# A second-layer weight pair loaded with unequal shares for the DMA engines

## The chip, the cores and the metric

The kernel runs on one core of a Trainium2 chip. The metric is the device time in microseconds (us) of one execution; for a kernel with several runs it is their median. A core has five engines that matter here: TensorE (PE; its weight loads are PEld), VectorE (DVE), ScalarE (ACT), GpSimd (POOL) and SyncE (SP), and sixteen DMA engines that move data between the chip's memory and the on-chip buffers. GpSimd and SyncE only issue the transfers here, apart from a few mask operations on GpSimd at the start.

## What is computed

Two layers follow each other. The first is attention over 8 batches, 8 heads, 576 positions and head dimension 64, with a window of 32 positions: the plain last 32 in heads 0 to 3, every fourth of the last 128 in heads 4 to 7. The second is a soft mixture of experts over the 4608 tokens that come out of it, with 8 experts of 4 slots:

```python
logits = x @ phi                          # 4608 x 32
d = softmax(logits, axis=0)               # over the tokens
slot_input = (d.T @ x).reshape(8, 4, 512)
for e in range(8):
    h = np.maximum(slot_input[e] @ w1[e], 0.0)     # w1[e]: 512 x 1024
    slot_out[e] = h @ w2[e]                        # w2[e]: 1024 x 512
c = softmax(logits, axis=1)               # over the slots
out = c @ slot_out.reshape(32, 512)       # 4608 x 512
```

All inputs and the output are f32 in memory. The weights w1 and w2 are 16.8 MB each, and q, k and v together 28.3 MB.

## The kernel before, in words

The program is a list of operations. Each names its engine, what it reads and writes, a cost and a key. A planner (`schedule`, lines 170 to 271) goes through them in its own modelled time, picks for each engine what can start first (the key decides between near ones), and so fixes the order of the instructions on every engine. The operations on GpSimd and SyncE keep the order in which the program lists them. `emit` (273 to 313) then writes the instructions, with semaphore waits where one engine needs another or a transfer. A DMA's semaphore is raised by each of the sixteen DMA engines, and a wait is for all of them (lines 303 to 307).

The attention is cut into eight units (two batches by four heads). A unit's q, k and v are loaded by six transfers of 32 rows (`load_unit`, line 411), into one of three staging buffers `stg`, with a cast from f32 to bf16 on the way. TensorE transposes them into `TT` (551 and 546), multiplies (589, 643), and VectorE and ScalarE work between. When a pair of units is through, the token logits (698), their exponentials and the slot sums (729, 746) follow.

The expert weights are loaded by `wload` (437 to 451), on GpSimd's queue as well, between and after the units. Their places: seven of the eight w1 matrices have buffers of their own (`WD`), the eighth and the w2 matrices go into staging buffers and `TT` as these come free. A w2 "pair" holds two experts: 128 rows (2 experts by 64 groups of 16 matrix rows), and in each row 16 x 512 f32 values that lie one after another in memory. The pairs are p0, p1, p2 and p3, the last cut by columns into p3a and p3b. GpSimd's order at the end is w15, w16, w17, p3a, p0, p1, p2, p3b (lines 760 to 788). Loads that reuse a buffer wait for TensorE to have read it.

p0 goes into `stg[:, 0, 0:8192]` (line 457). Line 449 cuts it into two loads of 128 rows by 4096 values:

```python
cut = [slice(0, 8), slice(8, 16)] if name == "p0" else [slice(None)]
```

After the last unit TensorE makes the slot inputs (798), the first expert layer (817), transposes (837), and the second layer (864), which takes the parts in the order p3a, p0, p1, p2, p3b, each waiting for its own load. Row sums (880) lie between p1 and p2. The result is scaled (891, 895), and the output is made tile by tile: TensorE multiplies (923, 925), VectorE and ScalarE scale out of PSUM (937, 938), and SyncE issues six output transfers (946). The first part of p0's buffer serves there as a staging tile (904 to 907).

Where the planner sees TensorE idle between the two times of `FILL` (line 24, in the planner's own us), it puts in filler: matmuls whose result nobody reads (`filler`, 950 to 966; line 955 in the profile), which keep TensorE busy.

Of the kernel before, what the change touches and what calls it, by code (L numbers as in the profile page):

```python
# [20 lines left out]
NU = 8  # L21
QB = 96
HALO = 32
FILL = (118, 148)


class DmaSem:
# [102 lines left out]
class Prog:  # L130
# [7 lines left out]
    def op(self, e, fn, r=(), w=(), a=(), alloc=(), cost=0.5, key=0.0, mode="f",  # L138
           sem=None, nbytes=0, nd=0, nq=1, ni=2, after=()):
        o = Op(e, fn, cost, key, mode)  # L140
        deps = list(after)
        for b in r:
            deps += b.ready
        for b in w:
            b.fresh()
            deps += b.prev
        for b in a:
            deps += b.prev
        seen = set()
        for d in deps:  # L150
            if d.id not in seen:
                seen.add(d.id)
                o.deps.append(d)
        for b in r:
            b.reads.append(o)
        for b in list(w) + list(a):
            b.ready.append(o)
        o.wr = [b for b in list(w) + list(a) if b.pool is not None]
        for b in list(r) + list(w) + list(a):
            if b.pool is not None and b not in o.touch:  # L160
                b.left += 1
                o.touch.append(b)
        o.alloc = list(alloc)
        o.sems = sem
        o.ni = ni + 2
        o.dma = nbytes / 435e3 + 0.011 * nd / 16 + 0.022 * nq
        self.ops.append(o)
        return o
# [147 lines left out]
def bass_dilated_sliding_attn__then__soft_moe_slots_kernel(  # L316
# [12 lines left out]
    op = P.op  # L329

    def sb(name, shape, dt=BF16):
        return A(nc.sbuf_tensor(name, shape, dt))
# [3 lines left out]
    stg = sb("stg", [128, 3, 9216])  # L336
# [22 lines left out]
    h_sb = sb("h_sb", [128, FF])  # L359
    hT = sb("hT", [128, 16, 128])  # L360
    half = sb("half", [128, 2, 32])
    so_sb = sb("so_sb", [128, DM])

    ps = A(nc.psum_tensor("ps", [128, 8, 512], F32))
# [19 lines left out]
    def pair(t):  # L384
        return ps[:, t.phys[0]:t.phys[0] + 2, :]
# [11 lines left out]
    b_stg = [Buf() for _ in range(3)]  # L397
# [5 lines left out]
    b_half = Buf()  # L403
    b_siT, b_h, b_hT, b_so = Buf(), [Buf(), Buf()], [Buf(), Buf()], [Buf(), Buf()]

    PACE = 8.26

    def due(u, x):
        return u * PACE + x

# [17 lines left out]
    HOME = {}  # L428
    b_home = []

    def home(ap, al, name):
        b = Buf()
        b.al = al
        HOME[name] = (ap, b)
        b_home.append((ap, b))

    def wload(name):
        ap, b = HOME[name]
        b.prev = [o for al in b.al for o in al.ready + al.reads]
        sem = DmaSem(nc, f"s_{name}")  # L440
        if name[:2] == "w1":
            src = moe_w1[int(name[2:])].rearrange("(p c) f -> p c f", c=4)
            dst = ap.rearrange("p (c f) -> p c f", c=4)
        else:
            g = int(name[1])
            c = {"": slice(0, 16), "a": slice(0, 8), "b": slice(8, 16)}[name[2:]]
            src = moe_w2[2 * g:2 * g + 2].rearrange("e (p c) f -> (e p) c f", c=16)[:, c, :]
            dst = ap.rearrange("p (c f) -> p c f", f=512)
        cut = [slice(0, 8), slice(8, 16)] if name == "p0" else [slice(None)]
        op("pool", lambda g: [g.dma_start(dst[:, x], src[:, x]) for x in cut], after=b.prev, a=[b],  # L450
           cost=0.6 * len(cut), sem=sem, nbytes=512 * ap.shape[1], nd=128 * len(cut), nq=len(cut))

# [1 line left out]
        home(WD[:, e, :], [], f"w1{e}")  # L454
    home(stg[:, 2, 0:4096], [b_stg[2]], "w17")
    home(stg[:, 2, 4096:8192], [b_stg[2]], "p3a")
    home(stg[:, 0, 0:8192], [b_stg[0]], "p0")
    home(stg[:, 1, 0:8192], [b_stg[1]], "p1")
    TTf = TT[:].rearrange("p a x -> p (a x)")
    home(TTf[:, 0:8192], b_TT, "p2")  # L460
# [35 lines left out]
    for i, t in enumerate(VNt):  # L496
# [6 lines left out]
       cost=0.1, key=1)  # L503
# [258 lines left out]
    for u in range(NU):  # L762
        for j in range(4):
            st_T(u, j)
        if u + 3 < NU:
            for n_ in W_AFTER.get(u + 2, ()):
                wload(n_)
            load_unit(u + 3)
        else:
            if u == 5:  # L770
                for n_ in W_AFTER[7]:
                    wload(n_)
            for n_ in {5: ["w17", "p3a"], 6: ["p0"], 7: ["p1"]}[u]:
                wload(n_)
        for i in range(6):
            st_S(u, i)
        for g in range(4):
            st_V(u, g)
        for g in range(4):
            st_P(u, g)  # L780
        for bpar in range(2):
            for x in range(2):
                st_X(u, bpar, x)
        if u % 2:
            for bpar in range(2):
                st_L(u - 1 + bpar, u)
# [25 lines left out]
    for hh in range(2):  # L812
        def pe(t, hh=hh):
            for c in range(4):
                for hi in range(2):
                    for j in range(4):
                        i_ = t.matmul(pair(hp)[32 * j:32 * j + 32, hh, :], siT[:, 512 * hi + 128 * c + 32 * j:
                                                       512 * hi + 128 * c + 32 * j + 32],
                                      w1v[2 * j + hi][:, c, 512 * hh:512 * hh + 512],
                                      start=(c == 0 and hi == 0), stop=(c == 3 and hi == 1))  # L820
            return i_
        ffn1 = op("pe", pe, r=[b_siT] + w1b, a=[hp], w=[b_hp[hh]], alloc=[hp] if hh == 0 else [],
                  cost=1.8, mode="c", key=K1, ni=64)
# [32 lines left out]
    PARTS = [("p3a", 3, 0, 8), ("p0", 0, 0, 16), ("p1", 1, 0, 16), ("p2", 2, 0, 16),  # L856
             ("p3b", 3, 8, 16)]
    for k_, (name, g, c0, c1) in enumerate(PARTS):
        wv = HOME[name][0].rearrange("p (c f) -> p c f", c=c1 - c0)
        for h_ in range(2):  # L860
            def pe(t, k_=k_, g=g, c0=c0, c1=c1, h_=h_, wv=wv):
                for c in range(c0, c1):
                    j = c % 4
                    i_ = t.matmul(pair(sp_)[32 * j:32 * j + 32, h_, 0:256],
                                  hT[:, c, 24 * g:24 * g + 32],
                                  wv[:, c - c0, 256 * h_:256 * h_ + 256],
                                  start=(k_ == 0 and c < c0 + 4), stop=(k_ == 4 and c >= c1 - 4))
                return i_
            last_ = op("pe", pe, r=b_hT + [HOME[name][1]], alloc=[sp_] if k_ == h_ == 0 else [],
                       a=[sp_, b_sp[h_]], cost=0.13 * (c1 - c0) / 4, mode="c",  # L870
                       ni=2 * (c1 - c0),
                       key=K1 + 2 + 0.5 * k_ + 0.1 * h_)
            if k_ == 2:
                mid = last_
    rs = tile(psum, 1)

    def rsum(t):
# [6 lines left out]
       after=[mid])  # L884
    op("dve", lambda vv: vv.reciprocal(rtok[:], bank(rs)[:, 0:N_TOK // 128]), r=[rs], w=[b_rtok],
       cost=0.2, key=K1 + 1)
# [23 lines left out]
    for o, (t0, n) in enumerate(TILES):  # L910
# [4 lines left out]
        for j0 in range(0, n, 2):  # L915
# [4 lines left out]
            for j in range(2 if split else min(2, n - j0)):  # L920
                def pe(t, o=o, po=po, j0=j0, j=j, split=split):
                    if split:
# [4 lines left out]
                p0 = op("pe", pe, r=(b_so[j:j + 1] if split else b_so) + b_expT, a=[po],  # L927
                        w=[b_po[j]], alloc=[po] if j == 0 else [], after=[p0] if j else [],
                        cost=0.12 if split else 0.22, key=kk + 0.01 * j)
                col = rcol[o] + (0 if split else j0 + j)  # L930

                def ev(en, po=po, ost=ost, j=j, j0=j0, split=split, col=col):
# [3 lines left out]
                    if en is nc.scalar:  # L936
# [3 lines left out]
                        cost=0.35 if split else 0.6, key=kk)  # L940
# [26 lines left out]

    P.schedule(filler, FILL)

# [39 lines left out]
```

## Time and profile before

| | |
|---|---|
| runs | 180.61, 179.62, 179.84, 179.72 us; median 179.78 |
| profiled execution | 180.1 us, of which the span of the profile is 178.3 |
| busy in the span | PE 137.1, DVE 112.6, ACT 96.1, POOL 34.4 us |
| DMA | 40.80 MB written at both ends, mean 229 GB/s; about 213 GB/s up to 145 us, 83 to 86 in the two slices from 147 to 156, 417 to 470 in the output |
| DMA queues (share of 16 engines) | GpSimd's 83.5%, SyncE's 12.8%, instructions 0.7% |
| chain that ended last, by engine | PE 38%, DMA 23%, DVE 20%, ACT 5%, issue 5% |
| costliest line of that chain | DMA into `TT` from w2, 18% |

Times count from the start of the profile's span. A group's row gives the line, the engine and the operation, what it writes and reads, how often, and in brackets how long the engine was idle before it and what ended that. The DMA share is the mean over the sixteen engines of the time that their packets took; as packets on one engine overlap a little, a full queue shows slightly over 1. GB/s are bytes as they arrive, so of the weights after the cast to bf16. "L864" is line 864 of the kernel before.

### The profile page before, as it was taken

Reading aid. Unit: us, or ns where it says so; the run is one execution under the profiler, and the core shown is the slowest. Engines: PE = TensorE matmul, PEld = TensorE weight load, DVE = VectorE, ACT = ScalarE, POOL = GpSimd, SP = SyncE. Lnnn points to the kernel's source line nnn. Section 1 sums busy time; section 2 is a strip of 40 time slices with the busy share of each in tenths; the row PEclk is TensorE's granted clock in tenths of the full one; section 3 lists DMA queues with packets and bytes.
Section 4 is the critical chain, followed back from the end, with each engine's and each line's share of the span. In section 5 each row is a group of like instructions: output and inputs, shape, how many; then the busy total and the mean of one; then the engine's idle time right before and its main releaser. Section 6 shows DMA issues by size and latency. Waiting matters only on the chain.

```text
span 178.3 us, 5800 instructions
## 1 busy us (share of the span) xinstructions
PE 137.1 (77%) x2615; PEld 106.0 (59%) x2621; DVE 112.6 (63%) x256; ACT 96.1 (54%) x141; POOL 34.4 (19%) x69
## 2 busy tenths in 40 slices
PE   0018898758999869999979899978999999897000
PEld 0018787646897758898869698755564785332000
DVE  6850688757687983798986898996330200699200
ACT  2006989465795953788965888872401000699000
POOL 7991707043005202600101001020000000000000
PEclk9999999995799995799996999996999999999655
DMA  5999999999999999999999999999999894299995
GB/s 81 209 213 209 217 215 214 217 210 214 213 219 213 216 210 213 220 212 215 210 223 212 215 211 222 209 215 237 202 228 228 191 215 86 83 417 453 458 470 235
DMA packets 5736, 40.80 MB, mean 229 GB/s; under 512 B 1616, under 2 KB 1616, under 8 KB 2000
## 3 DMA queue, kind: packets, MB, share of 16 engines
q0 software_dynamic: 4320, 30.94, 83.5%
q1 hardware_dynamic: 1392, 9.50, 12.8%
q8 instruction: 20, 0.33, 0.7%
q14 instruction: 4, 0.03, 0.0%
HBM read 61.93 MB, written 9.44 MB: 400 GB/s over the span
## 4 chain that ended last, share of the span: by engine, by line
PE 38%; DMA 23%; DVE 20%; ACT 5%; issue 5%; POOL 2%; DVEq 0%; POOLq 0%
DMA TT<-in_moe_w_dram 18%; PE ps L551 8%; PE ps L546 6%; DVE WD L938 5%; DMA stg<-in_v_dram 5%; PE ps L614 5%; PE ps L643 5%; PE ps L589 5%; DVE PT L604 4%; PE ps L698 4%; DVE XB L654 4%; PE ps L671 3%; DVE VN L619 3%; ACT TT L571 2%; ACT PT L596 2%
## 5 line engine op out<-in xcount | busy, mean ns | idle before, releaser
L596 ACT ACTIVATE PT<-ps 128x768 bf16<-128x768 f32 x48 | 37.1, 816 | 10.6 <-PE ps L589 10.3
L571 ACT ACTIVATE TT<-ps 128x864 f32<-128x864 f32 x32 | 28.5, 896 | 18.8 <-PE ps L551 16.0
L654 DVE TENSOR_TENSOR XB<-ps,RV 96x768 bf16<-96x768 f32 x32 | 30.4, 951 | 0.9
L551 PE MATMUL ps<-ident,stg 96*64 96x96 bf16 x576 | 17.9, 227 | 13.7 <-DMA stg<-in_v_dram 12.5
L551 PEld LDWEIGHTS ps<-ident,stg 96*64 96x64 bf16 x576 | 15.9, 126 | 15.0 <-DMA stg<-in_v_dram 12.5
L619 DVE COPY VN<-ps 128x768 bf16<-128x768 bf16 x32 | 17.1, 543 | 11.7 <-PE ps L614 11.7
L643 PE MATMUL ps<-VN,PT 128*128 128x65 bf16 x384 | 19.0, 200 | 3.8 <-issue 2.5
L589 PE MATMUL ps<-TT 64*128 64x96 bf16 x384 | 16.7, 215 | 5.1 <-issue 2.8
L643 PEld LDWEIGHTS ps<-VN,PT 128*128 128x128 bf16 x384 | 15.6, 102 | 5.1 <-issue 2.6
L614 PE MATMUL ps<-ident,TT 128*128 128x128 bf16 x192 | 17.4, 236 | 0.4 <-ACT PT L596 0.3
L421 POOL DMA_DIRECT2D stg<-in_q_dram x16 | 8.5, 541 | 43.3 <-PE ps L551 23.0
L589 PEld LDWEIGHTS ps<-TT 64*128 64x128 bf16 x384 | 10.4, 99 | 9.1 <-issue 3.1
L684 ACT ACTIVATE XT<-ps 128x576 bf16<-128x576 bf16 x22 | 13.7, 652 | 3.9 <-PE ps L671 3.9
L546 PE MATMUL ps<-ident,stg 96*128 96x96 bf16 x288 | 14.8, 206 | 0.3 <-DVE XB L654 0.3
L671 PE MATMUL ps<-ident,XB 96*128 96x96 bf16 x192 | 13.5, 216 | 1.1 <-DVE XB L654 0.9
L546 PEld LDWEIGHTS ps<-ident,stg 96*128 96x128 bf16 x288 | 13.2, 98 | 1.3 <-DVE XB L654 0.4
L614 PEld LDWEIGHTS ps<-ident,TT 128*128 128x128 bf16 x192 | 12.4, 106 | 2.7 <-ACT PT L596 0.5
L604 DVE TENSOR_TENSOR PT<-PT,mask_d 128x768 bf16<-128x768 bf16 x24 | 12.9, 545 | 1.1 <-ACT PT L596 1.0
L604 DVE TENSOR_TENSOR PT<-PT,mask_p 128x768 bf16<-128x768 bf16 x24 | 12.8, 551 | 1.1 <-ACT PT L596 0.7
L671 PEld LDWEIGHTS ps<-ident,XB 96*128 96x128 bf16 x192 | 10.5, 105 | 2.6 <-DVE XB L654 1.0
L955 PE MATMUL ps<-mask_p,ident 128*128 128x512 bf16 x39 | 10.5, 393 | 0.5 <-issue 0.4
L652 DVE RECIPROCAL RV<-ps 96x12 f32<-96x12 f32 x32 | 7.1, 223 | 5.8 <-PE ps L643 5.5
(81 smaller groups left out, 175.6 us busy)
## 6 DMA issues: line engine op xcount, KB each, us to landing
WD<-in_moe_w_dram POOLq DMA_DIRECT2D x7, 1024.0 KB, 30.3
stg<-in_q_dram POOLq DMA_DIRECT2D x16, 288.0 KB, 19.4
stg<-in_k_dram POOLq DMA_DIRECT2D x16, 288.0 KB, 21.1
stg<-in_v_dram POOLq DMA_DIRECT2D x16, 288.0 KB, 22.8
stg<-in_moe_w_dram POOLq DMA_DIRECT2D x4, 1024.0 KB, 28.2
out_dram<-WD SPq DMA_DIRECT2D x1, 4096.0 KB, 11.9
out_dram<-WD SPq DMA_DIRECT2D x1, 2304.0 KB, 7.5
stg<-in_moe_w_dram POOLq DMA_DIRECT2D x1, 2048.0 KB, 25.8
```

The lines of the kernel that those rows point to most:

```text
L546: i_ = t.transpose(bankb2(pt, a)[:, 96 * kk:96 * kk + 96], two[:, j // 2, c, :], ident[0:96, 0:96])
L551: i_ = t.transpose(bankb2(pt, a)[64 * hx:64 * hx + 64, 96 * kk:96 * kk + 96], src[:, hx, c, :], ident[0:96, 0:96])
L571: return ac.activation(d, sv, ACTF.Copy)
L589: i_ = t.matmul(pair(sc)[:, hx, QB * x:QB * x + QB], win(u, 1, h01, blk_, bpar)[64 * hx:64 * hx + 64], win(u, 0, h01, blk_, bpar)[64 * hx: ...
L596: op("act", lambda ac: ac.activation(sbt(pt)[:, 0:768].rearrange("p (x n) -> p x n", x=2), pair(sc)[:, :, 0:384], ACTF.Exp, scale=SCALE), ...
L604: return dv.tensor_tensor(p_, p_, m.unsqueeze(1).to_broadcast([128, 2, 384]), AluOp.mult)
L614: i_ = t.transpose(bankb(pv)[:, 128 * m:128 * m + 128], win(u, 2, h01, m, bpar), ident[:, :])
L619: op("dve", lambda dv: dv.tensor_copy(sbt(vn)[:, :, :, 0:64], bankb(pv)[:, 0:768].rearrange("p (m x d) -> p m x d", m=6, x=2)), r=[pv], w= ...
L643: i_ = t.matmul(pair(po)[:, bk, 65 * po_:65 * po_ + 65], sbt(pts[i])[:, o_:o_ + 128], sbt(vn)[:, m, half, 0:65], start=True, stop=True)
L654: op("dve", lambda dv: dv.tensor_tensor(sbt(xb)[:].rearrange("p m (x h d) -> p h x m d", x=2, h=2)[:, h01], pv()[:, :, :, 0:64], sbt(rv)[: ...
L671: i_ = t.transpose(bankb(px)[:, QB * m:QB * m + QB], sbt(xb)[:, m, 128 * x:128 * x + 128], ident[0:QB, 0:QB])
L684: return en.activation(d, s_, ACTF.Copy)
```

## The change

p0 is loaded by six transfers instead of two, all on the same semaphore, and its two halves lie in the buffer with a gap of 512 values between them, at 0 and at 4608, so that they stay two runs per row.

- rows 0 to 111: two loads of 112 rows by 4096 values, one for each half;
- a tiny load of 17 rows (`TURN`), two runs of 32 values each, into a buffer `scr` that nobody reads;
- rows 112 to 119, both halves (32 KB in each row);
- a tiny load of 8 rows into `scr`;
- rows 120 to 127, both halves.

The second layer's products of p0 read their columns 8 to 15 one place further on. `FILL` ends at 147 instead of 148. The costs given to the planner for this load are 3.6 us of GpSimd instead of 1.2. No other operation is changed.

```diff
-FILL = (118, 148)
+FILL = (118, 147)
...
+    scr = sb("scr", [32, 2, 2, 32])
...
+    TURN = 17
...
-        cut = [slice(0, 8), slice(8, 16)] if name == "p0" else [slice(None)]
+        if name == "p0":
+            src = src.rearrange("p (x c) f -> p x (c f)", x=2)
+            dst = ap.rearrange("p (x y) -> p x y", x=2)[:, :, 0:4096]
+
+            def skewed(g):
+                return [g.dma_start(dst[0:112, 0], src[0:112, 0]),
+                        g.dma_start(dst[0:112, 1], src[0:112, 1]),
+                        g.dma_start(scr[0:TURN, 0], src[0:TURN, :, 0:32]),
+                        g.dma_start(dst[112:120], src[112:120]),
+                        g.dma_start(scr[0:8, 1], src[0:8, :, 0:32]),
+                        g.dma_start(dst[120:128], src[120:128])]
+            op("pool", skewed, after=b.prev, a=[b], cost=3.6, sem=sem, nbytes=512 * 8192, nd=288,
+               nq=6)
+            return
+        cut = [slice(None)]
...
-    home(stg[:, 0, 0:8192], [b_stg[0]], "p0")
+    home(stg[:, 0, :], [b_stg[0]], "p0")
...
-        wv = HOME[name][0].rearrange("p (c f) -> p c f", c=c1 - c0)
+        wv = HOME[name][0].rearrange("p (c f) -> p c f", f=512)
...
-                                  wv[:, c - c0, 256 * h_:256 * h_ + 256],
+                                  wv[:, c - c0 + (1 if name == "p0" and c > 7 else 0), 256 * h_:256 * h_ + 256],
```

## Prediction

> **What bounds the kernel now.** I read the chain that ended last first, because it names the wait that sets the time. Its columns are start, length, what.
>
> ```profile
> 118.55 0.37 PE ps L589 x8
> 118.92 0.28 issue
> 119.20 0.52 POOL TT L450
> 119.72 32.49 DMA TT<-in_moe_w_dram
> 152.21 0.04 issue
> 152.26 0.43 PE ps L864 x8
> ```
>
> From 118.92 us the end is set by GpSimd's last weight load, p3b, which waits behind all earlier loads and lands at 152.21. TensorE starts the p3b products at 152.26. From there to the end (178.3) is 26.0 us of output work that the change does not touch.
>
> Next I read how full the DMA engines are, by stretch (columns: stretch, length, clock, DMA share, GB/s).
>
> ```profile
> 136.00:142.00 6.00, 1.00 1.02 218
> 142.00:146.00 4.00, 1.00 0.94 199
> 146.00:147.00 1.00, 1.00 0.90 188
> 147.00:148.00 1.00, 1.00 0.75 156
> 148.00:149.00 1.00, 1.00 0.63 131
> 149.00:150.00 1.00, 1.00 0.35 74
> 150.00:151.00 1.00, 1.00 0.22 49
> 151.00:152.00 1.00, 1.00 0.00 0
> ```
>
> The queue is full up to 146, then the sixteen engines run dry one after another until about 151. The load is not short of bandwidth at its end: its engines finish at different times. From 146 on the remaining work is 0.90+0.75+0.63+0.35+0.22 = 2.85 engine-us per engine, so all would end near 148.9 if they were even, against 150.8 or so for the last. Evening them out could bring at most about 1.9 us.
>
> The trace also keeps when each engine reports its share of p3b. Sorted: 147.85, 147.87, 147.88, 148.00, 148.08, 148.11, 148.36, 148.98, then a step, 150.30, 150.44, 150.47, 150.52, 151.03, 151.11, 151.52, 152.21. Eight early engines (mean 148.1), eight late ones (mean 150.95). Why eight? The DMA queues tell:
>
> ```profile
> q8 instruction: 20, 0.33, 0.7%
> ```
>
> Queue 8 carried 20 packets of 16 KB, on average 0.96 us each. At each of them exactly one engine's row of weight packets has a gap of that length, and their lengths repeat every eight packets (0.89, 0.9, 0.95, 1.0 to 1.2, 0.94, 1.0, 0.97, 0.96). So eight engines take turns: 20 x 0.96 / 8 = 2.4 us each, near the 2.8 us by which the late ones lag, four with three fetches and four with two.
>
> Last, TensorE's own order ahead of p3b (start, length):
>
> ```profile
> 146.94 3.18 PE L955 MATMUL ps<-mask_p,ident 128*128 128x512 bf16 x14
> 150.06 1.06 PE L864 MATMUL ps<-TT,hT 128*32 128x256 bf16 x32
> 151.05 0.82 PE L955 MATMUL ps<-mask_p,ident 128*128 128x512 bf16 x3
> 152.26 0.62 PE L864 MATMUL ps<-TT,hT 128*32 128x256 bf16 x16 [0.39 <-DMA TT<-in_moe_w_dram]
> ```
>
> L955 is filler. TensorE comes free at about 151.9, only 0.4 us before p3b lands. An earlier landing alone gains no more than that.
>
> [...] Nor does any view say which eight engines are the late ones.
>
> **The change part by part.**
>
> Bytes. Before, p0 is 16 rows of 16 KB (f32 source) for each engine. After, the two 112-row loads give 14 to each. If both 8-row loads fall on the same eight engines, these get 14 + 2 + 2 = 18 and the others 14. In the full stretch one such row takes 0.625 us and overlaps its successor by 0.02, so 0.61: eight engines end 2 x 0.61 = 1.21 us later, eight 1.21 us earlier. The total is unchanged.
>
> Why the tiny loads. [...] That is the skew; what it is worth depends on whether these are the early eight.
>
> Their own price. Thirty-four 128-byte reads lie on one engine. Nearest row: the phi load, 32 such packets per engine, whose packets run from 1.94 to 2.6, so about 0.65 us. [...] from below nothing, from above 0.65 us if that is already the latest engine. I take 0 on the path. Four more loads add four more completion packets of 22 ns per engine: 0.1 us on every engine, counted.
>
> GpSimd's queue. p0 now issues six loads, not two. One issue is 0.53 us:
>
> ```profile
> 97.29 1.07 POOL L450 DMA_DIRECT2D stg<-in_moe_w_dram  x2 [11.77 <-PE ps L551]
> 110.76 0.53 POOL L450 DMA_DIRECT2D stg<-in_moe_w_dram  x1 [12.40 <-PE ps L546]
> ```
>
> So 4 x 0.53 = 2.1 us more, behind 97.29, in the 12.40 us that GpSimd sits idle before p1 at 110.76; and the loads before p0 keep the engines busy until 113.9 or later. Cost nothing; it would cost only if p1's issue slipped beyond 123.6, where the first engine has finished p0. Nothing waits behind GpSimd but these loads, and SP is not touched.
>
> Filler. FILL ends one us earlier in the planner's time. The built order shows exactly one difference on TensorE: L955 before p2 goes from 15 to 16 matmuls, and the four between p2 and p3b are gone. By the row above (3.18 us for 15 issued) one is 0.21. TensorE thus reaches p3b at 150.06 + 0.21 + 1.06 = 151.3, not 151.9. ACT, DVE and SP have the same order. Filler removed could lower the clock at the tail; the clock stands at 1.00 through 152 and the gap is short, so 0. The products of p0 read a shifted column: the same 32 matmuls, 0.
>
> Sum if the skew fits: late engines 151.52 - 1.21 + 0.1 = 150.4, and 152.21 to 151.1 (this one also met the fetch at 150.18, which it would then miss); early ones 148.98 + 1.21 + 0.1 = 150.3. Everything has landed by 151.1, and TensorE at 151.3 becomes the bound: 152.26 - 151.3 = 0.95 us gained, no more, though the data are up to 1.8 us earlier. The profiled execution took 180.1 us (span 178.3 and 1.8 around it): 180.1 - 0.95 = 179.15. The median of the runs is 179.78, 0.3 less; I read that as p3b landing by 151.9 in most runs, where filler bounds. The end point (TensorE at 151.3) is then the same, so I do not subtract the 0.3: 179.1, a gain of 0.65 on the median.
>
> **The rivals.**
>
> Slower: the eight heavy engines include late ones. Place: p3b's landing. Price: a late engine with three fetches (151.03 to 152.21) that is made heavy ends 1.31 later, at 152.3 to 153.5. It decides as soon as one such engine is heavy, since one late engine delays the semaphore; if early and late engines alternate in number, every choice of eight neighbours has four late ones. For it: nothing in the trace ties the cursor's start to the early eight[...]. Against it: the late engines are exactly as many as the light ones, and if they are neighbours, a start can meet them all. Time: 180.1 + 0.1 to 1.3, less up to 0.3 for the median: 180.0 to 181.4, middle 180.8.
>
> No skew: the 8-row loads fall on different halves, or all on sixteen, or the tiny 8-row load does not turn the cursor. Then each engine gets 16 rows as before, plus 0.1 of completions: p3b at about 152.3, less filler in front; 179.8 to 180.2, middle 179.9. [...] Against it: 8 rows cannot fill 16 engines.
>
> A heavy late engine with only two fetches (150.3 to 150.5, then 151.6 to 151.8) lies between: 179.4 to 179.7. I count it with the first.
>
> **How the numbers follow.** The profile does not say where the cursor stands, so the first and the last case are near even; I put the first ahead because its gain needs only the filler to go and no three-fetch engine to be heavy. Skew fits, or nearly: 0.44 (178.7 to 179.6, most likely 179.1). No skew: 0.17. Skew against late engines: 0.39. About 0.5% (0.9 us: 178.88 and 180.68) is what a measurement of this kernel can tell from no change. Of the first case a third lies below 178.88: 0.14 faster. Of the slower case two thirds lie above 180.68: 0.26. The rest, 0.60, is within. The likeliest case's own range is 178.7 to 179.6; the range over the cases is 178.8 to 181.0, with about a tenth left out at each end.
>
> **What would show it.** Right: p3b's landings lose their step, the DMA share falls steeply between 149 and 151, TensorE starts L864's last group near 151.3 with no wait for the DMA. Wrong: p3b lands after 152.3 with a share that trails longer (late engines heavy), or the same eight-and-eight step (no skew). GpSimd's p1 issue should stay near 110.8, and queue 8 near 20 packets.

## The result, and the profile after

The change makes the kernel slower.

| | before | after |
|---|---|---|
| median | 179.83 us (55 runs) | 181.28 us (36 runs) |
| lowest to highest | 179.28 to 183.07 | 180.41 to 183.11 |
| profiled execution | 180.1, span 178.3 | 183.11, span 181.3 |

The ratio is 1.0081 [1.0065, 1.0096], so 1.45 us are lost. The profiled execution of the changed kernel is the slowest of its 36; the same kernel was profiled once more (`again`, below), at a time of 180.88 and a span of 179.2, and what follows says which readings the two share.

In this profile the chain of waits has the same form as before, with the last weight load later. Columns: start, length, what.

```profile
119.45 0.55 POOL TT L466
119.99 34.21 DMA TT<-in_moe_w_dram
154.21 0.04 issue
```

p3b is issued 0.27 us later than before and lands 2.0 us later, at 154.21. In `again` it lands at 152.94, 0.7 us later, and there the chain that ended last does not run over it at all, but over TensorE's own order (below).

The stretches of the changed kernel show where that comes from. Columns: stretch, length, clock, DMA share, GB/s.

```profile
136.00:142.00 6.00, 1.00 0.99 213
...
146.00:147.00 1.00, 1.00 1.06 221
147.00:148.00 1.00, 1.00 0.90 188
148.00:149.00 1.00, 1.00 0.81 172
149.00:150.00 1.00, 1.00 0.90 188
150.00:151.00 1.00, 1.00 0.36 74
151.00:152.00 1.00, 1.00 0.12 25
152.00:153.00 1.00, 1.00 0.16 33
153.00:154.00 1.00, 0.64 0.04 8
154.00:156.00 2.00, 0.50 0.00 0
```

Two things differ from before. The engines stay nearly full until 150, three us longer, and then there is still a tail: 25, 33 and 8 GB/s from 151 on are the last few engines (one alone moves 13.5: a packet of 8192 B every 0.606 us). The bytes say more than the shares. From 146 on 221 + 188 + 172 + 188 + 74 + 25 + 33 + 8 = 909 KB arrive, against 188 + 156 + 131 + 74 + 49 = 598 before. The 311 KB between them are 1.46 us at 213 GB/s: by 146 the changed kernel is about a microsecond and a half behind, although it loads the same weights. The skew only moves bytes from one engine to another and cannot do that.

The loss lies in one place. In the stretch in which the 8-row loads arrive, first the kernel before, then the changed one:

```profile
124.00:127.00 3.00, 0.82 1.07 227
```

```profile
124.00:127.00 3.00, 1.00 1.20 154
```

Before, 227 GB/s at a share of 1.07. After, 154 GB/s at a share of 1.20: the engines count as busy, but their packets take longer. A packet of 8 KB takes 0.625 us elsewhere and one of 16 KB 1.227; here single packets take up to 1.0 us more, and in `again` up to 1.2. Added over the stretch and divided by sixteen, this excess is 1.0 to 1.16 us per engine, against 0.01 in the kernel before. `again` shows it too (162 GB/s, 1.19).

The landings of p3b, one for each engine, in order. After: 147.67, 148.30, then twelve from 149.94 to 151.93, then 153.72 and 154.21. `again`: 147.78, 148.41, twelve from 150.14 to 152.13, then 152.93 and 152.94. The step between eight and eight is gone. Instead two engines run ahead and two lag, in both. The mean is 150.87 (150.82), against 149.55 before.

TensorE ahead of p3b in the changed kernel (start, length, what, idle time before it):

```profile
145.19 3.40 PE L971 MATMUL ps<-mask_p,ident 128*128 128x512 bf16 x15
149.38 1.06 PE L880 MATMUL ps<-TT,hT 128*32 128x256 bf16 x32 [0.79 <-DMA TT<-in_moe_w_dram]
154.25 1.05 PE L880 MATMUL ps<-TT,hT 128*32 128x256 bf16 x16 [3.81 <-DMA TT<-in_moe_w_dram]
```

TensorE is free at 150.44 and idles 3.81 us. Its clock falls meanwhile (0.64, then 0.50 in the stretches above), and the 16 products take 1.05 us, not 0.62. From their start to the end of the span it is 27.1 us, against 26.1 before: of the 3.0 us by which this execution is longer, 2.0 are the landing and 1.0 is this. In `again` TensorE itself comes last:

```profile
148.87 3.40 PE L971 MATMUL ps<-mask_p,ident 128*128 128x512 bf16 x15
152.20 1.49 PE L880 MATMUL ps<-TT,hT 128*32 128x256 bf16 x48
```

p2 had landed at 148.09, but TensorE still had row sums and the filler ahead of it, and it came to the last 16 products at 153.08, 0.14 us after p3b. The rest took 26.1. Its clock had been down earlier (0.57 from 124 to 128 us, against 1.00 in the first profile), which may be why it was late. Over all twenty profiles of this document TensorE is free for these products between 149.1 and 153.3 us, so whether it or the load decides differs from one execution to the next.

GpSimd's queue (start, length, what):

```profile
97.63 0.55 POOL L456 DMA_DIRECT2D stg<-in_moe_w_dram  x1 [13.40 <-PE ps L567]
...
100.80 0.55 POOL L461 DMA_DIRECT2D stg<-in_moe_w_dram  x1
111.00 0.58 POOL L466 DMA_DIRECT2D stg<-in_moe_w_dram  x1 [9.65 <-PE ps L562]
```

The six loads are issued by 101.35, and GpSimd idles 9.65 us before p1, which is issued at 111.00. That step was hidden. From the list of DMA queues:

```profile
q0 software_dynamic: 4992, 30.94, 83.2%
...
q8 instruction: 20, 0.33, 0.7%
```

The bytes are those of before, with 672 more packets on GpSimd's queue (4320 before).

### The profile page after: what moved, and what is told of

The parts are those of the page before. It is cut to its first block, busy times and chain, and to the rows that moved or that the text cites. A ratio compares the mean times of both kernels' runs of the same rounds, so it can differ in the third digit from the quotient of the medians.

```text
span 181.3 us, 5799 instructions
## 1 busy us (share of the span) xinstructions
PE 137.3 (76%) x2613; PEld 105.8 (58%) x2618; DVE 112.8 (62%) x256; ACT 95.7 (53%) x141; POOL 37.2 (20%) x73
## 4 chain that ended last, share of the span: by engine, by line
PE 39%; DMA 24%; DVE 19%; issue 5%; ACT 5%; POOL 2%; DVEq 0%; POOLq 0%
DMA TT<-in_moe_w_dram 19%; PE ps L567 9%; PE ps L562 6%; DMA stg<-in_v_dram 5%; PE ps L659 4%; DVE PT L620 4%; DVE WD L954 4%; PE ps L605 4%; PE ps L630 4%; DVE XB L670 4%; PE ps L714 4%; DVE VN L635 3%; PE ps L687 3%; ACT TT L587 2%; ACT PT L612 2%
## 5 line engine op out<-in xcount | busy, mean ns | idle before, releaser
L567 PE MATMUL ps<-ident,stg 96*64 96x96 bf16 x576 | 19.6, 237 | 14.5 <-DMA stg<-in_v_dram 12.6
L567 PEld LDWEIGHTS ps<-ident,stg 96*64 96x64 bf16 x576 | 17.4, 133 | 15.9 <-DMA stg<-in_v_dram 12.6
L605 PE MATMUL ps<-TT 64*128 64x96 bf16 x384 | 16.2, 209 | 5.8 <-issue 3.6
L630 PE MATMUL ps<-ident,TT 128*128 128x128 bf16 x192 | 16.3, 226 | 0.7 <-ACT PT L612 0.4
L630 PEld LDWEIGHTS ps<-ident,TT 128*128 128x128 bf16 x192 | 11.5, 101 | 2.8 <-ACT PT L612 0.5
L941 PE MATMUL ps<-so_sb,expT 128*128 128x512 bf16 x34 | 10.9, 454 | 0.3 <-DVE stg L954 0.2
L954 DVE TENSOR_SCALAR WD<-ps,rtok 128x512 f32<-128x512 f32 x15 | 10.1, 745 | 0.2
## 6 DMA issues: line engine op xcount, KB each, us to landing
stg<-in_q_dram POOLq DMA_DIRECT2D x16, 288.0 KB, 19.6
```

What stands on the lines that cost most here:

```text
L567: i_ = t.transpose(bankb2(pt, a)[64 * hx:64 * hx + 64, 96 * kk:96 * kk + 96], src[:, hx, c, :], ident[0:96, 0:96])
L605: i_ = t.matmul(pair(sc)[:, hx, QB * x:QB * x + QB], win(u, 1, h01, blk_, bpar)[64 * hx:64 * hx + 64], win(u, 0, h01, blk_, bpar)[64 * hx: ...
L630: i_ = t.transpose(bankb(pv)[:, 128 * m:128 * m + 128], win(u, 2, h01, m, bpar), ident[:, :])
L954: return en.tensor_scalar(d_, s_, sc_, None, op0=AluOp.mult)
```

## The experiments

**What was measured.** Apart from the time, one number was read from each profile: the mean over the engines of p1's landing less the mean of p3a's. p3a is the load before p0, p1 the one after it, so this is what p0 and p1 together cost an engine: 19.6 us in the kernel before (32 rows of 16 KB at 0.61), 20.8 in the changed kernel. Being a mean, it does not see how rows are dealt out, only lost time. "Ahead" and "behind" count the engines whose share of p3b lands well before or well after the rest. Ratios are to the kernel before on the same chip. Diffs are against the changed kernel where nothing else is said.

**First four: which part of the change costs?** `tiny_only` keeps the two tiny loads and the filler's end, and loads p0 in two halves of 128 rows:

```diff
-                        g.dma_start(dst[0:112, 0], src[0:112, 0]),
-                        g.dma_start(dst[0:112, 1], src[0:112, 1]),
+                        g.dma_start(dst[:, 0], src[:, 0]),
+                        g.dma_start(dst[:, 1], src[:, 1]),
                         g.dma_start(scr[0:TURN, 0], src[0:TURN, :, 0:32]),
-                        g.dma_start(dst[112:120], src[112:120]),
-                        g.dma_start(scr[0:8, 1], src[0:8, :, 0:32]),
-                        g.dma_start(dst[120:128], src[120:128])]
+                        g.dma_start(scr[0:8, 1], src[0:8, :, 0:32])]
```

> The changed kernel with even shares: both big loads of p0 have 128 rows again, the two 8-row loads of 32 KB rows are gone, the tiny loads of 17 and 8 rows stay. Theory (three terms: tiny loads, late engines made heavy, a slower TensorE after a long wait): the trace of the changed kernel shows 622 more 4-byte packets at the tiny loads than before, and all engines late by about 1 us afterwards, so p3b lands 0.6 to 1.0 us later than before on all engines, 180.3 to 181.0. Rival 1 (only the unequal shares cost): as before or a little faster for the shorter filler, 179.2 to 179.9.

Measured: 179.99 against 179.92, 0.9991 [0.9972, 1.0011]. p1 less p3a 19.8, p3b's last landing 152.12. In the stretch in which p0 arrives no packet is stretched (excess 0.01 us):

```profile
124.00:127.00 3.00, 1.00 1.02 203
```

That the tiny loads themselves lose the time does not hold: 180.3 to 181.0 had been expected. They do explain the packets. Of the 672 new ones, 50 are data (34 + 16) and 64 completions (4 loads by 16, most of 22 ns). The other 558 have 4 bytes each. Their number comes out if they lie on the engines that a load does not use: 15 x 34 for the 17-row load, and 8 x 2 for each of the three 8-row loads. The same count gives 74 for `turn3` and 50 for `turn15`, below, and their traces have as many (each 160 packets more than before: 22 of data, 64 completions and 74, and 46, 64 and 50). So the counts say that 17 rows go to one engine, 8 rows to eight, 3 to three and 15 to fifteen; the loads of 112 rows add none of these packets and use all sixteen. All of the tiny loads together cost 0.2 to 0.3 us in the mean landings and nothing that the time shows.

`no_tiny` is the other half: both tiny loads go, the 8-row loads stay.

```diff
-                        g.dma_start(scr[0:TURN, 0], src[0:TURN, :, 0:32]),
...
-                        g.dma_start(scr[0:8, 1], src[0:8, :, 0:32]),
```

> The changed kernel without both tiny loads: two loads of 112 rows, two of 8 rows. Theory: the second 8-row load takes the other eight engines, so shares are even, and the 4-byte packets are nearly gone: p3b lands within 0.2 us of before, 179.3 to 180.0. If 112 or 8 rows cost by themselves (another rival): 180.5 or more. If the cursor does not advance, both 8-row loads meet on one half and p3b's landings show a skew as in the changed kernel: 180.5 to 181.3.

Measured: 180.82, 1.0042 [1.0022, 1.0062]; p1 less p3a 20.1, excess in the packets 0.59 us per engine. That miss was the first useful one. Without the tiny loads p3b's last share lands at 152.56, not at 154.21, as if the two 8-row loads fell on different halves and each engine had 16 rows again; still 0.4% is lost, and the packets stretch. So the 8-row loads cost something without any skew.

`after_fill148` and `fill147` part the filler from the rest: the first is the changed kernel with the old end of the filler, the second the kernel before with the new one.

```diff
-FILL = (118, 147)
+FILL = (118, 148)
```

> The changed kernel with FILL ending at 148 as before, so that three or four filler matmuls run again between p2 and p3b. Theory: the loads land as in the changed kernel; TensorE waits 0.7 us less idle, its clock falls less, 0.1 to 0.6 us faster than the changed kernel: 180.6 to 181.2. Rival 1 (late landing alone): equal to the changed kernel, 181.2 to 181.4. Rival 2 (the shortened filler is the whole loss): 179.8.

Measured: 181.59, 1.0084 [1.0058, 1.011], so not faster than the changed kernel's 1.0081.

```diff
-FILL = (118, 148)
+FILL = (118, 147)
```

> The kernel before with FILL ending at 147. Theory: p3b's landing bounds, so within 0.2 us of before, 179.6 to 180.0. Rival 2 (the shortened filler is the whole loss, by a lower clock in the output part): 180.5 to 181.3. Forecast's reading that filler bounds most runs of before: 179.2 to 179.5.

Measured: 179.86, 1.0002 [0.9979, 1.0025]. A matmul of filler more or less neither made the loss nor saves anything. The prediction's reading that the filler bounds most runs of the kernel before falls with it: 179.2 to 179.5 would have been due.

**Next four: which engines are heavy, and can the loads be spread?** The prediction and the expectations call the engine at which a short load begins the cursor. No view names an engine, so where it stands can't be read; that each row of the first tiny load moves the heavy block on by one of sixteen places is the author's assumption, tested by the landings of these runs alone. `turn3` and `turn15` change the number of those rows.

```diff
-    TURN = 17
+    TURN = 3
```

> The changed kernel with TURN 3 (a 3-row tiny load). In both profiles of the 17-row form p3b's landings show two engines well ahead and two well behind the other twelve, as if six early and two late engines were heavy. Theory (the eight early engines are neighbours and the block stands two places beside them): a turn of 3 or of 15 meets all eight early ones, the other meets four. If 3 is the right one: no two stragglers, p3b about 0.9 us earlier than with 17, 180.0 to 180.7; if the wrong one: four of each, 181.2 to 181.9. Rival (the early engines are no neighbours, or the cursor differs from one execution to the next): as with 17, 181.2 to 181.5.

Measured: 181.35 against 180.10, 1.0050 [1.0023, 1.0077]; four engines ahead, four behind, p3b last at 153.28; p1 less p3a 20.3, excess 0.8.

```diff
-    TURN = 17
+    TURN = 15
```

> The changed kernel with TURN 15. Theory: the mirror of the run with 3: one of the two has all eight early engines heavy (180.0 to 180.7), the other four (181.2 to 181.9). Rival: as with 17.

Measured: 181.42, 1.0061 [1.0038, 1.0084]; two ahead, two behind, p3b last at 153.55; p1 less p3a 20.6, excess 1.0. Had the early engines been eight neighbours that 17 rows miss by two places, one of 15 and 3 should, on that assumption, have met all eight. Neither did, so they are not neighbours.

`spread` gives every engine the same bytes, but writes the two small loads into partitions that lie apart.

```diff
-                return [g.dma_start(dst[0:112, 0], src[0:112, 0]),
-                        g.dma_start(dst[0:112, 1], src[0:112, 1]),
+                return [g.dma_start(dst[r::8], src[r::8]) for r in range(7)] + [
                         g.dma_start(scr[0:TURN, 0], src[0:TURN, :, 0:32]),
-                        g.dma_start(dst[112:120], src[112:120]),
+                        g.dma_start(dst[7::16], src[7::16]),
                         g.dma_start(scr[0:8, 1], src[0:8, :, 0:32]),
-                        g.dma_start(dst[120:128], src[120:128])]
+                        g.dma_start(dst[15::16], src[15::16])]
```

> The changed kernel, same bytes for every engine and same turn, but with other rows in the loads: seven loads of 16 rows (every eighth), both halves each, then the tiny load, rows 7, 23, ... 119, the tiny load, rows 15, 31, ... 127. Theory ([...] in the runs so far the mean time from p3a's to p1's landing was 19.6 us before, 19.8 with the tiny loads alone, 20.1 with the two 8-row loads alone, 20.8 in the changed kernel): spread over the partitions that excess goes, p1's mean landing is 19.6 to 20.0 after p3a's, and the time is 0.5 to 1.0 us below the changed kernel, 180.2 to 180.8. Rival (any load on eight engines costs that, or the skew does): 20.6 or more, 181.2 to 181.5.

Measured: 181.12, 1.0045 [1.0021, 1.0068]; the excess is halved (0.48 us, p1 less p3a 20.4). Two engines are ahead, two behind.

`again` is the changed kernel unaltered, for a second profile.

> The changed kernel once more, for its profile. Theory (the cursor starts at one place in every execution): p3b's landings show two engines ahead and two behind again, 181.0 to 181.5. Rival (the cursor stays from one execution to the next [...]): another number of stragglers, zero to eight.

Measured: 180.94, 1.0045 [1.0019, 1.0072]. On this chip the change costs a little less, and `spread`, beside it, cannot be told from it. That experiment leaves the question open.

**Next four: is it the place they write to?** In the changed kernel each of the two 8-row loads writes 128 KB into eight neighbouring partitions, and the excess is 1.0 to 1.16 us per engine; in `tiny_only`, with the tiny loads and without these two, it is 0.01. No view shows how the buffer takes writes, so what remains is to vary the rows. The size is not the same everywhere: `no_tiny` and `turn3` write into the same partitions and lost 0.59 and 0.8, and `spread`, whose rows lie sixteen apart, lost 0.48.

`ports8` gives the same engines the same shares, in partitions that lie four apart. Three loads of 32 rows are followed by four of 8 rows, each into every fourth partition; by the author's count of places the first, third and fourth of these fall on the heavy eight, the second on the others (12 + 6 rows of 16 KB, and 12 + 2).

```diff
-                return [g.dma_start(dst[0:112, 0], src[0:112, 0]),
-                        g.dma_start(dst[0:112, 1], src[0:112, 1]),
+                return [g.dma_start(dst[r::4], src[r::4]) for r in range(3)] + [
                         g.dma_start(scr[0:TURN, 0], src[0:TURN, :, 0:32]),
-                        g.dma_start(dst[112:120], src[112:120]),
+                        g.dma_start(dst[3:32:4], src[3:32:4]),
+                        g.dma_start(dst[35:64:4], src[35:64:4]),
+                        g.dma_start(dst[67:96:4], src[67:96:4]),
                         g.dma_start(scr[0:8, 1], src[0:8, :, 0:32]),
-                        g.dma_start(dst[120:128], src[120:128])]
+                        g.dma_start(dst[99:128:4], src[99:128:4])]
```

> Same shares (18 and 14 rows of 16 KB) and the same turn of 17, but the rows of every 8-row load lie four partitions apart: three loads of 32 rows (every fourth), then loads of rows 3, 7, ... 31; 35, ... 63; 67, ... 95; 99, ... 127, the third of five turns being the tiny one's neighbour, so that one half gets three of the four. Theory [...]: the excess is gone, p1 lands on average 19.7 to 20.0 us after p3a (before 19.6, changed kernel 20.8, spread 20.4), two stragglers remain; 180.0 to 180.6. Rival (any data load on eight engines stalls the others): 20.5 or more, 181 or more.

Measured: 180.67 against 180.37, 1.0005 [0.9978, 1.0033]; p1 less p3a 19.9, no excess:

```profile
124.00:127.00 3.00, 1.00 1.11 227
```

`dst_near` is its counterpart. It reads rows that lie apart, but writes them where the changed kernel does; sixteen partitions thus hold other rows of the weights.

```diff
-                        g.dma_start(dst[112:120], src[112:120]),
+                        g.dma_start(dst[112:120], src[3:32:4]),
                         g.dma_start(scr[0:8, 1], src[0:8, :, 0:32]),
-                        g.dma_start(dst[120:128], src[120:128])]
+                        g.dma_start(dst[120:128], src[67:96:4])]
```

> The changed kernel, except that the two 8-row loads read other rows of the weights (3, 7, ... 31 and 67, 71, ... 95) into the same eight neighbouring partitions; so it computes with wrong rows of w2 in 16 partitions. Theory (the write side): p1's mean landing stays at 20.6 to 20.9 after p3a and the time at 180.9 to 181.5. Rival (reads of eight neighbouring rows of memory): 19.8 to 20.1, 180.0 to 180.6.

Measured: 181.55, 1.0085 [1.0049, 1.0122]; p1 less p3a 20.8, excess 1.16:

```profile
124.00:127.00 3.00, 1.00 1.16 151
```

Writing four partitions apart takes the stall away (no excess), reading rows that lie apart does not (1.16 us): the place of writing is the cause. The two stand side by side on one chip, 0.88 us apart, and their intervals do not meet. `spread` lies between them, with rows sixteen apart and half of the stall (0.48), so the distance alone does not order the three cases: 1.16 side by side, none at four apart, 0.48 at sixteen. Why was not shown.

`ports8_t0` is `ports8` without the 17-row load.

```diff
-                        g.dma_start(scr[0:TURN, 0], src[0:TURN, :, 0:32]),
```

> As the run with rows four partitions apart, without the 17-row load, so the block of heavy engines starts at the cursor itself. Turns of 15 and of 17 each showed two engines ahead in p3b's landings, 3 showed four, so a turn of 0 should leave at most one or two. Theory: mean as in that run or 0.1 less, at most one straggler, p3b at 151.2 to 152.3, 179.3 to 180.0: at best a little under the kernel before. Rival: two stragglers as with 17, 180.0 to 180.6.

Measured: 180.62, 1.0017 [0.9992, 1.0042]; p1 less p3a 19.7; two ahead, two behind, p3b last at 152.63. At most one laggard had been expected.

`rows16` has no skew and no tiny load; the last 16 rows of both halves are one load, over all sixteen engines, into neighbouring partitions.

```diff
-                        g.dma_start(scr[0:TURN, 0], src[0:TURN, :, 0:32]),
-                        g.dma_start(dst[112:120], src[112:120]),
-                        g.dma_start(scr[0:8, 1], src[0:8, :, 0:32]),
-                        g.dma_start(dst[120:128], src[120:128])]
+                        g.dma_start(dst[112:128], src[112:128])]
```

> No load on eight engines and no tiny load: two loads of 112 rows and one of rows 112 to 127 on all sixteen engines, even shares. Theory (neighbouring partitions, not the number of engines): [...] p1's mean landing 20.0 to 20.3 after p3a, as without the tiny loads (20.1), 180.3 to 180.9. Rival (loads on eight engines): 19.6, 179.6 to 180.0.

Measured: 180.92, 1.0044 [1.0025, 1.0062]; p1 less p3a 19.8, excess 0.21, p3b last at 152.06. Here the load lands as early as before, and the time is still 0.4% longer. The excess is much smaller than the 1.16 of `dst_near`, though here sixteen neighbouring partitions are written. That the engines don't all come to this load at the same time may be why; it was not tried. So these runs show where the stall arises, and not what sets its size. In the profile of `rows16` the loss is on TensorE (stretch; busy time of PE, PEld, DVE, ACT, POOL; clock; DMA share; GB/s):

```profile
150.00:152.00 2.00, 0.00 (x0) 0.00 (x0) 0.00 (x0) 0.00 (x0) 0.00 (x0) 1.00 0.16 33
152.00:154.00 2.00, 1.30 (x19) 0.80 (x21) 0.95 (x2) 0.73 (x2) 0.00 (x0) 0.69 0.00 0
154.00:156.00 2.00, 2.00 (x5) 0.69 (x5) 1.64 (x4) 1.46 (x3) 0.00 (x0) 0.50 0.35 131
```

TensorE is through with all else at 149.2, waits 2.88 us, and its clock falls to 0.50. From the start of p3b's products to the end of the span it is 26.65 us. How the length of the wait goes with the rest, in these profiles: with 3.6 to 3.8 us of waiting the rest took 27.0 to 27.1 in three profiles, and with 1.84 or less 26.1 in all. With 2.75 to 2.95 the clock fell to 0.50 in the stretch after the wait, and the rest took 26.6 to 26.7 in four profiles, while `spread` waited 3.12 and took 26.1. So these waits give no sharp limit. Whether this makes the whole of `rows16`'s 0.4% was not tried.

**Last six: the right engines.** Four starts of a block of eight were known by now. Let place 0 be where the block begins with no turn. If each row of the turn moves it on by one place of sixteen, TURN = 17 makes places 1 to 8 heavy, and 15, 3 and no turn begin at places 15 (or -1), 3 and 0. Counting the engines ahead (early and light) gives 6, 6, 4 and 6 early engines in the four blocks. Several sets of eight early places fit that; a block of six was to narrow it down. In `six`, six engines get 18 rows or more (four of them 20) and ten get 14.

```diff
-                return [g.dma_start(dst[0:112, 0], src[0:112, 0]),
-                        g.dma_start(dst[0:112, 1], src[0:112, 1]),
+                return [g.dma_start(dst[r::4], src[r::4]) for r in range(3)] + [
+                        g.dma_start(dst[3::8], src[3::8]),
                         g.dma_start(scr[0:TURN, 0], src[0:TURN, :, 0:32]),
-                        g.dma_start(dst[112:120], src[112:120]),
-                        g.dma_start(scr[0:8, 1], src[0:8, :, 0:32]),
-                        g.dma_start(dst[120:128], src[120:128])]
+                        g.dma_start(dst[7:55:8], src[7:55:8]),
+                        g.dma_start(scr[0:10, 1], src[0:10, :, 0:32]),
+                        g.dma_start(dst[55:103:8], src[55:103:8]),
+                        g.dma_start(scr[16:26, 1], src[0:10, :, 0:32]),
+                        g.dma_start(dst[103::8], src[103::8])]
```

> Heavy loads on six neighbouring engines only, after a turn of 17, rows apart so that they do not stall: three loads of 32 rows, one of 16, then 6, 6 and 4 rows, with tiny loads of 10 rows between them that bring the cursor back. Four engines carry 20 rows of 16 KB, two 18, ten 14. Theory (the two late engines of the blocks at turns 15, 0 and 17 stand at the edges, and engines 1 to 6 from the cursor are all early): no stragglers, p3b at 150.8 to 151.5, then TensorE's own order bounds: 179.2 to 179.9, up to 0.4 us under the kernel before on the same chip. Rival (the late ones stand inside): stragglers later than before by 1.2 to 2.4, p3b at 153.5 to 154.5, 180.8 to 181.8.

Measured: 180.43 against 180.05, 1.0019 [0.9994, 1.0044]; p1 less p3a 19.9; four ahead, two behind, where no laggard had been expected.

`six_fill145` is the same with a shorter filler.

```diff
-FILL = (118, 147)
+FILL = (118, 145)
```

> The same with FILL ending at 145, five filler matmuls fewer ahead of p2's products (11, not 16). Theory: if p3b lands by 151, TensorE is free for it 1.0 us earlier and the time falls by up to 0.3 us more, 178.9 to 179.8. Rival (a late p3b or a lower TensorE clock after a longer wait): as the run with FILL 147 or up to 0.6 us slower.

Measured: 180.85, 1.0035 [1.0008, 1.0062]; p3b last at 153.06. The filler is no help while two engines lag.

`ports8_t14` is `ports8` with another turn.

```diff
-    TURN = 17
+    TURN = 14
```

> Rows four apart, shares 18 and 14, TURN 14, that is two places back. Turns of 15, 0 and 17 showed two early engines outside the block, so 14 can show one to three. Theory: one straggler at best or three, p3b at 152.3 to 153.0, 179.9 to 180.6. Rival (another cursor start than in the runs before): none or more than three.

Measured: 180.78, 1.0032 [1.0006, 1.0059]; two ahead, two behind, so, by the same count, six of places -2 to 5 are early. Of all sets of eight places just three fit these six settings (TURN 17, 15, 3, 14, none, and the block of six), and in none of them are eight neighbours early. One, the set -1, 0, 1, 2, 3, 4, 7 and 8, has six: -1 to 4. That is where `six` comes to lie with 15 rows in the first tiny load; by the two other sets one of those six would still be late. `six_t15`, against `six`:

```diff
-    TURN = 17
+    TURN = 15
```

> Six heavy engines as before, after a turn of 15 instead of 17. From the numbers ahead and behind at turns 14, 15, 0, 3, 17 and in the six-engine runs (two late with 18 rows, four early ahead), the early engines should be those at -1, 0, 1, 2, 3, 4, 7 and 8 places from the cursor's start, so a turn of 15 puts all six heavy shares on early ones. Theory: two engines ahead, none behind, p3b at 150.6 to 151.6 in place of 152.8, 0.5 to 1 us less than with the turn of 17 and 0.2 to 0.5 us less than the kernel before on the same chip, where TensorE does not bound. Rival: stragglers again, p3b at 152.5 or later, as with 17.

Measured: 179.16 against 180.39, 0.9943 [0.9921, 0.9965]; two ahead, none behind. Its stretches and the start of p3b's products:

```profile
148.00:149.00 1.00, 1.00 0.86 180
149.00:150.00 1.00, 1.00 0.50 107
150.00:151.00 1.00, 1.00 0.05 8
```

```profile
151.22 0.62 PE L882 MATMUL ps<-TT,hT 128*32 128x256 bf16 x16 [0.22 <-DMA TT<-in_moe_w_dram]
```

The share drops from 0.86 to 0.05 within two us: the last engines finish nearly together, p3b lands at 151.18, a microsecond earlier than before, and TensorE waits 0.22 us for it. It is now as late as the load.

`six_t15_f145`, on the same chip, therefore ends the filler earlier as well, and `fill145`, without the skew and with runs of its own of the kernel before, is its control.

```diff
-FILL = (118, 147)
+FILL = (118, 145)
-    TURN = 17
+    TURN = 15
```

> The same with FILL ending at 145 (11 filler matmuls ahead of p2's products, not 16). Theory: with p3b at 150.6 to 151.6 TensorE is free for it when it lands; up to 0.3 us less than with FILL 147. Rival (a cooler TensorE after the wait, or TensorE's own order late for other reasons): the same or up to 0.5 us more.

Measured: 178.96 against 180.39, 0.9915 [0.9889, 0.9941]. All has landed at 150.90, and the products follow one another without a wait for a DMA; p3b's are the last third of the x48 and begin near 151.05 (150.18 + 1.49 - 0.62):

```profile
147.71 2.53 PE L973 MATMUL ps<-mask_p,ident 128*128 128x512 bf16 x11
150.18 1.49 PE L882 MATMUL ps<-TT,hT 128*32 128x256 bf16 x48
```

`fill145` is an edit of the kernel before:

```diff
-FILL = (118, 148)
+FILL = (118, 145)
```

> The kernel before with FILL ending at 145 and even shares: the control for the six-engine run at turn 15 with the same filler, which took 0.9915 of the kernel before. Theory (the unequal shares made the gain, by an earlier p3b): p3b lands at 151.6 to 152.3 as before and the time is 0.998 to 1.003 of the kernel before. Rival (the shorter filler made it): 0.990 to 0.994.

Measured: 180.28 against 180.09, 1.0002 [0.9979, 1.0026]. The filler alone brings nothing; a skew that puts the rows on the right engines, and apart in the buffer, gains 0.6%, and 0.9% with the shorter filler. The two intervals overlap, so what the filler adds is not settled, but both versions are faster than the kernel before. In the profile of `fill145` p3b had landed at 151.80 and TensorE came to its products at 153.25, so that execution was TensorE's.

## Why the prediction was wrong

Predicted 179.1 (178.8 to 181.0), most likely no measurable change; measured 181.28. By its own steps:

- **"The total is unchanged."** This step failed, and most of the loss is its (0.80 of 0.85% on the chip that ran `ports8` and `dst_near`). The bytes are unchanged, the time that the engines need for them is not: two loads of eight rows into eight neighbouring partitions stretch the packets by 1.0 to 1.16 us per engine. The mean landing of p3b moved from 149.55 to 150.87, of which 0.3 is the tiny loads' (`tiny_only`, 149.87). The step took 0.61 us for every row; it is right for rows that are written four partitions apart (`ports8`, without excess), and the price of writing into neighbouring ones was not asked for. `ports8` and `dst_near` tell the cause from all else: the same engines, the same rows per engine, 1.0005 against 1.0085.
- **"If the skew fits."** That both 8-row loads would meet the same eight engines was an assumption: no view of before shows how short loads are dealt. The landings agree with it, for they lose their eight-and-eight step (two ahead at 147.67 and 148.30, twelve together, two behind). But by these landings six of the eight are early ones and two are late, in every profile in which eight engines are heavy after a turn of 17. No turn could have done better than six, by any of the three sets that fit. The two heavy late engines are, by this reading, the last landings of both profiles (153.72 and 154.21; 152.93 and 152.94).
- **The slower rival** named heavy late engines, p3b's landing as the place and a time of 180.0 to 181.4, and the measured time lies in its range. It had the chance 0.39 and should have been ahead: an unknown start out of sixteen, with one late engine enough to spoil it, is worse than near even. But its mechanism by itself is not what was measured. In `ports8` the same two engines lag and the ratio is 1.0005 [0.9978, 1.0033], in `ports8_t14` two lag and it is 1.0032. That its range holds the measured time is luck in part: the stall is missing from it, and from the whole forecast, whose range for that reason ended 0.3 us too low.
- **A start that moves on** from one execution to the next, the rival of `again`, did not hold in the profiles: the start fits one place in every one of them. The times of `six_t15_f145` speak for the executions without a profile. Its short loads have 15 + 10 + 10 + 6 + 6 + 4 = 51 rows, three more than three times sixteen, so a start that moved on by them would soon have made late engines heavy; but its 15 times lie between 178.64 and 179.89, where `six_fill145`, with two of them, ranges from 179.62 to 181.95.
- **"So 0" for the clock at the tail.** Right in `again`, wrong by 1.0 us in the first profile, where TensorE waited 3.81 us. In the median this can be a part only, since the runs differ in how long TensorE waits.
- **TensorE free by 151.3**: this took one execution for all. It was 150.44 in the first profile, where it decided nothing, and 153.08 in `again`, where it decided. In `six_t15`, where the load is early, the bound of the prediction's sum shows: TensorE is free at 151.00 and starts p3b's products at 151.22.
- **The issues on GpSimd** (111.00 for p1 against 110.76), **the filler** (one matmul more ahead of p2, 15 in the trace against 14, and no four before p3b) and **queue 8** (20 packets) came as predicted. **The tiny loads' own price** was put at 0.1 us on every engine and was 0.2 to 0.3 in the mean; the 558 packets on idle engines were not foreseen, but the time does not show them.

The parts add up about so: stall alone, evenly dealt, 1.0042 (`no_tiny`); misplaced rows alone 1.0005 to 1.0032 (the three `ports8` kernels); both 1.0045 to 1.0085 (`again`, `turn15`, the changed kernel, `dst_near`); neither 0.9991 (`tiny_only`). The intervals of a single chip are too wide to say more exactly how the 0.8% is divided.

## What to carry to other kernels

A load cut into few rows is not the same load in smaller pieces: ask which engines carry it, into which partitions it writes and whether these are neighbours, and see in a trace whether its packets take longer before calling the total unchanged. To give slow engines less work, first find out which they are, one by one; eight neighbours that hold six of the right ones are worse than no skew, a skew on six engines, all of them right ones, gained 0.6%. A mean over the engines and the last landing answer different questions: the first shows lost time, the second shows who got it.

## What the runs showed that had not been expected

- Writing from eight engines into eight neighbouring partitions held up other engines' packets as well. In the changed kernel the first of p1's packets, of 16 KB, starts at 122.52 us, while the other engines are still at p0 (14 of p0's packets under way at 123.0). The nine of p1's that start from 125 to 126 us, while the last 8-row loads still arrive, take 1.84 us on average and not 1.23, and p1's packets make up nearly half of the excess (0.50 of 1.07 us).
- A load that uses one or eight engines puts a 4-byte packet on each idle engine for each packet of data of an active one, 558 of them here; the counts of `turn3` and `turn15` follow the same rule.
- If a row of the turn is a place, the eight early engines stand at places -1 to 4, 7 and 8; that is inferred from the landings of the skewed kernels, and `six_t15` (two ahead, none behind) agrees. They are known by their landings only: that these are the engines without the packets of the instruction queue is inferred from the prediction's count of gaps, eight engines in turn, and no view lists it. That the start is the same in each profiled execution is seen, not why.
- The clock fell in two profiles with no long wait: in `fill145` TensorE was busy nearly throughout (1.92 and 2.00 of 2 us) and yet stood at 0.76 from 148 to 150 us and at 0.50 from 150 to 152, in `ports8_t0` at 0.55 and 0.59 from 146 to 150. In `fill145` ten filler matmuls took 3.90 us meanwhile, where eleven took 2.53 in `six_t15_f145`, and TensorE came last. Such drops add to the spread of the runs; what triggers them stays open.
